# Ten dense weight units prepared in the experts and six in the dense stage, with two `sq` buffers, a later cast and three raw buffers

## The chip, the cores and the metric

The kernel runs on one core of one Trainium2 chip. The metric is device time in microseconds (us); below, a row's start is counted from the first instruction of the profiled execution. TensorE does the matrix products; VectorE, ScalarE and GpSimd the elementwise work; SyncE (SP) issues most transfers.

## What is computed

Three layers in a row, float32 results of shape (3072, 384): a gated linear attention over 4 x 8 heads, a mixture of eight experts of which each token goes to one, and a dense block with squared ReLU.

```python
for t in range(S):                                   # attention, per head
    state = alpha[:, :, t, :, None] * state + einsum('bhd,bhe->bhde', k[:, :, t], v[:, :, t])
    y[:, :, t] = einsum('bhd,bhde->bhe', q[:, :, t], state)
e_idx = argmax(x @ w_gate, axis=1)                   # experts, x is (3072, 384)
h = maximum(x[mask] @ w1[e], 0.0)                    # w1 (8, 384, 1024)
out[mask] = gate_w[mask, None] * eom[mask, e, None] * (h @ w2[e])
h = maximum(x @ w_in, 0.0)                           # dense, w_in (384, 2048)
out = (h * h @ w_out).astype(float32)                # w_out (2048, 384)
```

`w_in` and `w_out` arrive as float64 and are turned into pairs of float32 parts by integer operations in the kernel.

## The kernel before

Products that need more than one pass are made of three matmuls (`three`): both operands are split into a high part and a low part. Three stages follow each other on TensorE: the attention (to about 170 us), the experts (to 404 us) and the dense block.

The **experts** are 64 units, eight for each expert (`NU = E * NF`). In pass n of the loop TensorE runs `up1(n)` (the `ha` matmuls) and then `down1` of unit n-1 (the `acc` matmuls). ScalarE makes `hh` (L700) and VectorE `hl` (L703) from `ha`; `down1(n)` needs both. `fetch` brings a unit's raw weights by two transfers on SP's queue (L159, L160) into one of four raw buffers; `parts(m)` splits them by a cast on ScalarE (L170) and a subtraction on GpSimd (L171). Pass n prepares unit n+3 and then fetches the unit four behind that one, into the buffer that GpSimd has just read.

The **dense block** is 16 weight units over six blocks of 512 tokens. Since not all 16 units are ready when it starts, its passes are dealt to stretches (`SEGS`): block 0 with the first `NE` units, block 1 with all 16, block 0 with the rest, then blocks 2 to 5. Pass i of the loop runs `up2` (nine `ha` matmuls; then ScalarE's `r`, VectorE's `r`, ScalarE's `hh`, VectorE's `hl`, L928 to L934) and `down2` of pass i-2 (twelve `acc` matmuls). `split` makes the `xh` and `xl` of the next stretch (L913, L914): two of three at the middle of a stretch, the third in its last pass, on the queues ahead of that pass's `r`. At the end of the stretch over block 0, `finished` copies the four sums to `half` (L944, L946).

A dense unit is made ready by `dense_steps`, a generator of 18 steps: for each of two halves a load of `bits` (on SP's queue, two buffers) and eight steps of `wide_steps`, with one square and one cast on ScalarE (L1344, L1355) and seven VectorE operations (L1346 to L1363). The instructions are queued in the order of the program, and each engine works through its own queue in order. The generator `dense` prepares the first `NE` units: from pass 6 of the experts on, 18 x `NE` steps are dealt evenly to 57 passes, at the end of each. `late` prepares the others in the dense loop, between `up2` of pass i and `down2` of pass i-2, spread evenly over the first 22 passes (`need`).

Of the kernel before, what the change touches and what calls it, by code (L numbers as in the profile page):

```python
# [9 lines left out]
F32 = mybir.dt.float32  # L10
# [17 lines left out]
def moe_block_kernel(ctx: ExitStack, tc: tile.TileContext, q, k, v, alpha, w_gate, w_ogate,  # L28
                     w1, w2, w_in, w_out, out, dbg=None):
    nc = tc.nc  # L30
    B, H, S, D = q.shape
    NT, DM = out.shape
    E, _, FF = w1.shape
    FF2 = w_in.shape[1]
    P = 128
# [5 lines left out]
    NF2 = FF2 // P  # L41
    XW = 2 * D
    NU = E * NF
    GROUPS = [6, 6, 6, 3, 1, 1, 1]
    NRA = 4
    NRB = NF2 - 3
    NE = NF2 // 2
    BLK = 512
    NB = NT // BLK
    LAST = 2  # L50
    AHEAD = 6
# [11 lines left out]
    raw_p = fast.enter_context(tc.tile_pool(name="raw", bufs=2))  # L63
# [4 lines left out]
    with tc.manual_schedule():  # L68
# [66 lines left out]
        def source(n):  # L135
            if n < NU:
                e, f = divmod(n, NF)
                a, b = (w[bass.ds(expert[e], 1)].squeeze(0) for w in (w1, w2))
            else:
                f = n - NU  # L140
                a, b = w_in, w_out
            return (a[:, f * P:(f + 1) * P].rearrange("(k p) f -> p k f", p=P),
                    b[f * P:(f + 1) * P, :])
# [7 lines left out]
        def fetch(n):  # L151
            cols, rows_ = source(n)
            if n < NRA:
                if n % 2 == 0:
                    raws["pair"] = ring_b.tile([P, 4, DM], F32R, tag="w", name="raw").bitcast(F32)
                raw = raws["pair"][:, n % 2 * 2:n % 2 * 2 + 2, :]
            else:
                raw = (m2 if n % 4 >= 2 else raw_p).tile([P, 2, DM], F32, tag="raw", name="raw")
            nc.sync.dma_start(out=raw[:, 0, :].rearrange("p (k f) -> p k f", k=NK), in_=cols)  # L159
            nc.sync.dma_start(out=raw[:, 1, :], in_=rows_)  # L160
            raws[n] = raw
# [12 lines left out]
        def dense_steps(pool, first, last):  # L174


            halves = [(n, j) for n in range(first, last) for j in range(2)]
            loaded = {}

            def bring(i):  # L180
                if i < len(halves):
                    n, j = halves[i]
                    src = source(n)[j]
                    if w_in.dtype == F32:
                        raw = dst = pool.tile([P, DM], F32, tag="bits", name="bits")
                    else:
                        raw = pool.tile([P, DM, 2], I32, tag="bits", name="bits")
                        dst = raw.rearrange("p f o -> p (f o)")
                        src = src.bitcast(I32)
                    if j == 0:  # L190
                        dst = dst.rearrange("p (k f) -> p k f", k=NK)
                    nc.sync.dma_start(out=dst, in_=src)
                    loaded[i] = raw

            bring(0)
            for i, (n, j) in enumerate(halves):
                bring(i + 1)
                yield
                w = (unit_tile(n) if j == 0 else ring[n])[:, 2 * j:2 * j + 2, :]
                raw = loaded.pop(i)  # L200
                if w_in.dtype != F32:
                    yield from wide_steps(nc, pool, w, raw)
                    continue
                nc.scalar.copy(w[:, 0, :], raw)
                yield
                nc.vector.tensor_tensor(out=w[:, 1, :], in0=raw, in1=w[:, 0, :].bitcast(F32),
                                        op=ALU.subtract)
                yield
# [523 lines left out]
        def run(steps):  # L732
            for step in steps:
                step()
# [65 lines left out]
        i = NCH - 2  # L800
# [5 lines left out]
        for i, g in moving:  # L806
            x = xn.pop(i)
            nc.vector.tensor_scalar(x, x, g, None, op0=ALU.mult)
            scatter("xs", xs, idx[:, i:i + 1], x)
        i = NCH - 1  # L810
# [66 lines left out]
        m1 = moe.enter_context(tc.tile_pool(name="m1", bufs=1))  # L877
        m2 = moe.enter_context(tc.tile_pool(name="m2", bufs=2))
# [39 lines left out]

        SEGS = [(0, range(NE)), (1, range(NF2)), (0, range(NE, NF2))]
        SEGS += [(j, range(NF2)) for j in range(2, NB)]  # L920
# [54 lines left out]
        for n in range(NRA + 2, AHEAD + 2):  # L975
            fetch(n)
# [50 lines left out]

        dense = dense_steps(m2, NU, NU + NE)
        late = dense_steps(m2, NU + NE, NU + NF2)
        STEPS = 18  # L1030
# [3 lines left out]
        for n in range(NU):  # L1034
            e, f = divmod(n, NF)
            if f == 0 and e + 1 < E:
                choose(e + 1)
                gather(e + 1)
                if e == 0:
                    fetch(AHEAD + 2)  # L1040
                    fetch(AHEAD + 3)
            if f == 0 and e:
                offv[e] = nc.values_load(offi[0:1, e:e + 1], engines=[ACT], min_val=0,
                                         max_val=NT)
            if f == NF - 2:
                for kk in range(NK - 1):
                    if e + 1 < E:
                        turn(e + 1, kk)
                    else:
                        split(0, kk)  # L1050
            c = slice(EARLY if n < AHEAD else 0, WIDTHS[e])
            run(up1(n, c))
            if f == NF - 1:
                if e + 1 < E:
                    turn(e + 1, NK - 1)
            if n:
                down1(*last)
                m = n + NRA - 1 + sum(n < x for x in pauses)
                if n not in pauses and m < NU:
                    parts(m)  # L1060
                    if m + 4 < NU:
                        fetch(m + 4)
            last = n, c
            if n < NF - 2:
                for kk in range(NK):
                    part = slice(n * XP // (NF - 2), (n + 1) * XP // (NF - 2))
                    nc.gpsimd.memset(x2[:, kk, part], 0.0)
            if n == 2:
                next(dense)
            if n == 1:  # L1070
                sort()
            if n % 2 and n >= NU - 2 * NCH:
                i = (n - NU + 2 * NCH) // 2
                scatter("idl", idl, idx[:, i:i + 1], tok[:, i:i + 1])
            if n == 4:
                badb = judge()
            if n == 6:
                verdict(badb)
            if n >= AHEAD:
                k0, k1 = (STEPS * NE * (x - AHEAD) // (NU - 1 - AHEAD) for x in (n, n + 1))  # L1080
                for _ in itertools.islice(dense, k1 - k0):
                    pass
# [6 lines left out]


        seq = [(g, f) for g, (_, fs) in enumerate(SEGS) for f in fs]
        need = SEGS[0][1].stop + NF2 - 2
        for i, (g, f) in enumerate(seq):
            fs = SEGS[g][1]
            more = g + 1 < len(SEGS)
            if f == fs[len(fs) // 2] and more:
                for kk in range(NK - 1):
                    split(g + 1, kk)
            up2(g, f)
            if i < need:  # L1100
                k0, k1 = (STEPS * (NF2 - NE) * x // need for x in (i, i + 1))
                for _ in itertools.islice(late, k1 - k0):
                    pass
            if more or f < NF2 - LAST:
                if i > 1:
                    down2(*seq[i - 2])
# [232 lines left out]
def wide_steps(nc, pool, w, raw):  # L1339


    lo, hi = raw[:, :, 0], raw[:, :, 1]
    sq = pool.tile([w.shape[0], w.shape[2]], F32, tag="sq", name="sq", bufs=1)
    nc.scalar.activation(sq, hi.bitcast(F32), AF.Square)  # L1344
    yield
    nc.vector.scalar_tensor_tensor(out=hi.bitcast(F32), in0=sq, scalar=2.0 ** -30,  # L1346
                                   in1=hi.bitcast(F32), op0=ALU.is_ge, op1=ALU.mult)
    yield
    t = sq.bitcast(I32)
    nc.vector.tensor_scalar(t, hi, 3, 0x3FFFF000, op0=ALU.logical_shift_left, op1=ALU.bitwise_and)  # L1350
    yield
    nc.vector.scalar_tensor_tensor(out=t, in0=hi, scalar=-0x40000000, in1=t, op0=ALU.bitwise_and,
                                   op1=ALU.bitwise_or)
    yield
    nc.scalar.copy(w[:, 0, :], sq)  # L1355
    nc.vector.tensor_scalar(hi, hi, 0x1FF, 11, op0=ALU.bitwise_and, op1=ALU.logical_shift_left)
    yield
    nc.vector.scalar_tensor_tensor(out=lo, in0=lo, scalar=21, in1=hi, op0=ALU.logical_shift_right,
                                   op1=ALU.bitwise_or)
    yield  # L1360
    nc.vector.tensor_scalar(hi, t, -0x800000, None, op0=ALU.bitwise_and)
    yield
    nc.vector.scalar_tensor_tensor(out=w[:, 1, :], in0=lo, scalar=2.0 ** -31, in1=hi.bitcast(F32),  # L1363
                                   op0=ALU.mult, op1=ALU.mult)
    yield
# [31 lines left out]
```

## Time and profile before

| | |
|---|---|
| three runs | 831.48, 834.2, 836.35 us; median 834.2 |
| profiled execution | 830.97 us, span from first to last instruction 829.2 us |
| TensorE busy | 796.7 us (96%), 5215 matmuls |
| VectorE busy | 498.4 us (60%) |
| ScalarE busy | 381.3 us (46%) |
| GpSimd busy | 228.6 us (28%) |
| granted TensorE clock | 0.989 of full speed in the mean |

A row's time is from one execution. Matmuls are pipelined: the durations of neighbours overlap, and TensorE's pace is read from their starts. In brackets at the end of a row stand the idle time of the engine before that instruction and what ended it.

### The profile page before, as it was taken

The numbers are of one execution on the slowest core, as the hardware profiler recorded it, in microseconds if no ns is written. First come the engines' busy times: TensorE is split into PE (matmuls) and PEld (weight loads), VectorE is DVE, ScalarE is ACT, GpSimd is POOL, SyncE is SP. The second block draws the span as 40 slices with busy tenths as digits, with TensorE's granted clock in tenths as the row PEclk, the third lists the DMA queues.
The fourth block names the chain that finished last, engine by engine and source line by source line (L and its number), as shares of the span: only waits on it lengthen the run. The fifth ranks groups of instructions, "written<-read, shape, count | busy, mean of one in ns | idle before, by whom it ended". The sixth has DMA issues, their size and how long they took to land.

```text
span 829.2 us, 14100 instructions
## 1 busy us (share of the span) xinstructions
PE 796.7 (96%) x5215; PEld 731.1 (88%) x5215; DVE 498.4 (60%) x969; ACT 381.3 (46%) x734; POOL 228.6 (28%) x275
## 2 busy tenths in 40 slices
PE   7999999899999999999997999999999999999995
PEld 5899998798899999999986997999999999999995
DVE  8889999857355645876687787443333333333331
ACT  3677777554454555555444344332333333333221
POOL 3002341628456766777200000210002002002002
PEclk9999999899999999999998999999999999999998
DMA  9999994544554655674112110000000000000001
GB/s 135 179 210 180 209 175 99 185 132 157 156 161 128 182 149 152 167 181 127 39 58 76 58 58 21 39 13 27 0 1 39 1 1 38 1 1 39 1 0 42
DMA packets 153860, 74.98 MB, mean 90 GB/s; under 512 B 105406, under 2 KB 149430, under 8 KB 153782
## 3 DMA queue, kind: packets, MB, share of 16 engines
q1 hardware_dynamic: 149878, 64.52, 35.1%
q0 software_dynamic: 3904, 9.47, 3.1%
q8 instruction: 43, 0.70, 0.4%
q14 instruction: 35, 0.29, 0.1%
HBM read 61.76 MB, written 12.20 MB: 89 GB/s over the span
## 4 chain that ended last, share of the span: by engine, by line
PE 44%; issue 32%; DVE 14%; ACT 4%; POOL 3%; DMA 1%; SPq 1%; ACTq 0%; POOLq 0%; DVEq 0%
PE ha L1334 5%; PE ha L1336 5%; PE acc L1335 5%; PE acc L1334 5%; PE ha L1335 5%; PE acc L1336 5%; PE tr L268 3%; PE fx L425 2%; PE y L404 2%; POOL out_dram L129 2%; PE sc L337 2%; DVE r L929 2%; PE y L400 2%; ACT hh L933 2%; DVE bits L1346 1%
## 5 line engine op out<-in xcount | busy, mean ns | idle before, releaser
L1334 PE MATMUL ha<-xh,w 128*128 128x512 f32 (+7 forms) x456 | 173.9, 381 | 4.4 <-ACT xh L913 4.4
L1335 PE MATMUL ha<-xl,w 128*128 128x512 f32 (+7 forms) x456 | 172.3, 378 | 1.0 <-DVE xl L914 1.0
L1336 PE MATMUL ha<-xh,w 128*128 128x512 f32 (+7 forms) x456 | 172.5, 378 | 0.0
L929 DVE SCALAR_TENSOR_TENSOR r<-ha,r 128x512 f32<-128x512 f32 x96 | 66.3, 690 | 139.9 <-ACT r L928 137.6
L171 POOL TENSOR_TENSOR w<-raw,w 128x768 fp32r<-128x768 f32 x60 | 112.4, 1873 | 76.9 <-ACT w L170 73.9
L1334 PE MATMUL acc<-w,hh 128*128 128x384 f32 x384 | 130.6, 340 | 2.4 <-ACT half L946 1.8
L129 POOL DMA_INDIRECT out_dram<-o,ids x24 | 24.5, 1021 | 392.4 <-ACT o L954 359.8
L1336 PE MATMUL acc<-w,hl 128*128 128x384 f32 x384 | 130.6, 340 | 0.1
L1335 PE MATMUL acc<-w,hh 128*128 128x384 f32 x384 | 130.4, 340 | 0.0
L928 ACT ACTIVATE r<-ha 128x512 f32<-128x512 f32 x96 | 57.2, 596 | 144.4 <-PE ha L1336 144.3
L934 DVE TENSOR_TENSOR hl<-r,hh 128x512 fp32r<-128x512 f32 x96 | 66.6, 693 | 66.3 <-ACT hh L933 48.5
L1334 PEld LDWEIGHTS ha<-xh,w 128*128 128x128 f32 x456 | 85.9, 188 | 14.4 <-ACT xh L913 5.2
L1336 PEld LDWEIGHTS ha<-xh,w 128*128 128x128 f32 x456 | 85.8, 188 | 14.0
L933 ACT CAST hh<-r 128x512 fp32r<-128x512 f32 x96 | 59.5, 620 | 83.8 <-DVE r L929 82.6
L1335 PEld LDWEIGHTS ha<-xl,w 128*128 128x128 f32 x456 | 85.9, 188 | 11.6 <-DVE xl L914 1.9
L1334 PEld LDWEIGHTS acc<-w,hh 128*128 128x128 f32 x384 | 72.7, 189 | 7.3 <-ACT half L946 2.2
L170 ACT CAST w<-raw 128x768 fp32r<-128x768 f32 x64 | 53.5, 836 | 55.5 <-PE acc L1336 39.4
L1335 PEld LDWEIGHTS acc<-w,hh 128*128 128x128 f32 x384 | 72.7, 189 | 3.9
L1336 PEld LDWEIGHTS acc<-w,hl 128*128 128x128 f32 x384 | 72.7, 189 | 0.4 <-DVE hl L934 0.4
L703 DVE SCALAR_TENSOR_TENSOR hl<-ha,hh 128x448 fp32r<-128x448 f32 (+7 forms) x58 | 33.6, 580 | 54.8 <-ACT hh L700 52.3
L1334 PE MATMUL acc<-hh,w 128*128 128x448 f32 (+7 forms) x174 | 61.4, 353 | 0.0
L1335 PE MATMUL acc<-hl,w 128*128 128x448 f32 (+7 forms) x174 | 60.8, 350 | 0.1
(215 smaller groups left out, 1317.9 us busy)
## 6 DMA issues: line engine op xcount, KB each, us to landing
raw<-in_moe_w_dram SPq DMA_DIRECT2D x128, 192.0 KB
bits<-in_moe_w_in_dram SPq DMA_DIRECT2D x16, 384.0 KB
bits<-in_moe_w_out_dram SPq DMA_DIRECT2D x16, 384.0 KB
nat_al<-in_alpha_dram SPq DMA_DIRECT2D x24, 192.0 KB
nat_k<-in_k_dram SPq DMA_DIRECT2D x24, 192.0 KB
nat_q<-in_q_dram SPq DMA_DIRECT2D x24, 192.0 KB
nat_v<-in_v_dram SPq DMA_DIRECT2D x24, 192.0 KB
gx<-xs SPq DMA_DIRECT2D x22, 192.0 KB
```

The source lines that it names most:

```text
L129: ins = nc.gpsimd.indirect_dma_start(out=dst[:, :], out_offset=bass.IndirectOffsetOnAxis(ap=ix, axis=0), in_=src, in_offset=None)
L170: nc.scalar.copy(w[:, 0::2, :], raw)
L171: engine.tensor_tensor(out=w[:, 1::2, :], in0=raw, in1=w[:, 0::2, :].bitcast(F32), op=ALU.subtract)
L268: nc.tensor.transpose(ps[:, pr, :], src[:, pr, :], ident)
L703: nc.vector.scalar_tensor_tensor(out=hl, in0=ps, scalar=0.0, in1=hh.bitcast(F32), op0=ALU.max, op1=ALU.subtract)
L928: nc.scalar.activation(r, ps, AF.Relu)
L929: nc.vector.scalar_tensor_tensor(out=r, in0=ps, scalar=0.0, in1=r, op0=ALU.max, op1=ALU.mult)
L933: nc.scalar.copy(hh, r)
L934: nc.vector.tensor_tensor(out=hl, in0=r, in1=hh.bitcast(F32), op=ALU.subtract)
L1334: nc.tensor.matmul(ps, st[0], mv[0], start=start, stop=False)
L1335: nc.tensor.matmul(ps, st[0], mv[1], start=False, stop=False)
L1336: nc.tensor.matmul(ps, st[1], mv[0], start=False, stop=stop)
```

## The change

`NE`, the number of dense units prepared in the experts, goes from 8 to 10, and six are left to the dense loop. Their steps are dealt to 21 of the first 24 dense passes; passes 9, 10 and 11 (the end of the first stretch and the two behind it) get none. `sq` takes its pool's two buffers instead of one. The cast of `sq` to the weight's high part is queued two steps later. There are three raw buffers instead of four: two in `raw_p` and one in `m1`; the fetch goes three units ahead, and pass 0 fetches one unit less.

```diff
-    NE = NF2 // 2
+    NE = NF2 - 6
...
-                raw = (m2 if n % 4 >= 2 else raw_p).tile([P, 2, DM], F32, tag="raw", name="raw")
+                raw = (m1 if (n - NRA) % 3 == 2 else raw_p).tile([P, 2, DM], F32, tag="raw", name="raw")
...
                 if e == 0:
                     fetch(AHEAD + 2)
-                    fetch(AHEAD + 3)
...
                     parts(m)
-                    if m + 4 < NU:
-                        fetch(m + 4)
+                    if m + 3 < NU:
+                        fetch(m + 3)
...
-        need = SEGS[0][1].stop + NF2 - 2
+        spare_at = [i for i in range(NE + NF2 - 2) if i not in (NE - 1, NE, NE + 1)]
...
             up2(g, f)
-            if i < need:
-                k0, k1 = (STEPS * (NF2 - NE) * x // need for x in (i, i + 1))
+            if i in spare_at:
+                x = spare_at.index(i)
+                k0, k1 = (STEPS * (NF2 - NE) * y // len(spare_at) for y in (x, x + 1))
                 for _ in itertools.islice(late, k1 - k0):
                     pass
...
-    sq = pool.tile([w.shape[0], w.shape[2]], F32, tag="sq", name="sq", bufs=1)
+    sq = pool.tile([w.shape[0], w.shape[2]], F32, tag="sq", name="sq")
...
-    nc.scalar.copy(w[:, 0, :], sq)
     nc.vector.tensor_scalar(hi, hi, 0x1FF, 11, op0=ALU.bitwise_and, op1=ALU.logical_shift_left)
     yield
     nc.vector.scalar_tensor_tensor(out=lo, in0=lo, scalar=21, in1=hi, op0=ALU.logical_shift_right,
                                    op1=ALU.bitwise_or)
     yield
+    nc.scalar.copy(w[:, 0, :], sq)
     nc.vector.tensor_scalar(hi, t, -0x800000, None, op0=ALU.bitwise_and)
```

## Rows read from the trace of the kernel before

**Rows 1.** Stretches: TensorE, its weight loads, VectorE, ScalarE, GpSimd; clock, DMA.

```profile
360.00:400.00 40.00, 39.95 (x232) 39.56 (x232) 31.27 (x44) 21.22 (x38) 29.62 (x28) 1.00 0.51 137
400.00:440.00 40.00, 36.40 (x176) 31.34 (x174) 28.73 (x57) 17.44 (x33) 1.59 (x2) 0.99 0.20 50
520.00:560.00 40.00, 40.00 (x202) 36.23 (x202) 18.29 (x29) 14.33 (x25) 7.50 (x13) 1.00 0.07 30
```

**Rows 2.** TensorE's timeline, dense stage: start, duration, line, operation, idle before it.

```profile
410.39 0.34 PE L1334 MATMUL acc<-w,hh 128*128 128x384 f32 x1
...
427.97 0.44 PE L1334 MATMUL acc<-w,hh 128*128 128x384 f32 x1 [0.60 <-ACT hh L933]
...
439.03 0.79 PE L1334 MATMUL ha<-xh,w 128*128 128x512 f32 x1 [2.71 <-ACT xh L913]
...
453.88 0.45 PE L1334 MATMUL acc<-w,hh 128*128 128x384 f32 x1 [1.81 <-ACT half L946]
...
513.92 0.50 PE L1334 MATMUL ha<-xh,w 128*128 128x512 f32 x1 [1.66 <-ACT xh L913]
...
519.47 0.34 PE L1334 MATMUL acc<-w,hh 128*128 128x384 f32 x1
...
527.87 0.34 PE L1334 MATMUL acc<-w,hh 128*128 128x384 f32 x1
```

**Rows 3.** One stretch with a lower clock, columns as in rows 1.

```profile
439.00:445.90 6.90, 6.14 (x17) 5.35 (x18) 5.76 (x11) 2.74 (x6) 0.00 (x0) 0.51 0.18 57
```

**Rows 4.** VectorE's timeline, dense stage: first `r`, a split, one whole half.

```profile
407.02 0.69 DVE L929 SCALAR_TENSOR_TENSOR r<-ha,r 128x512 f32<-128x512 f32 x1 [4.72 <-ACT r L928]
...
439.81 0.69 DVE L914 TENSOR_TENSOR xl<-x,xh 128x512 fp32r<-128x512 f32 x1
...
454.73 0.69 DVE L929 SCALAR_TENSOR_TENSOR r<-ha,r 128x512 f32<-128x512 f32 x1 [0.38 <-ACT r L928]
456.11 0.69 DVE L934 TENSOR_TENSOR hl<-r,hh 128x512 fp32r<-128x512 f32 x1 [0.69 <-ACT hh L933]
456.72 0.55 DVE L1346 SCALAR_TENSOR_TENSOR bits<-sq,bits 128x384 f32<-128x384 f32 x1
...
459.69 0.56 DVE L1363 SCALAR_TENSOR_TENSOR w<-bits 128x384 fp32r<-128x384 int32 x1
460.16 0.68 DVE L929 SCALAR_TENSOR_TENSOR r<-ha,r 128x512 f32<-128x512 f32 x1
```

**Rows 5.** ScalarE's timeline at the end of the first dense stretch.

```profile
437.94 0.51 ACT L1355 CAST w<-sq 128x384 fp32r<-128x384 f32 x1 [1.62 <-DVE sq L1352]
438.36 0.61 ACT L913 CAST xh<-x 128x512 fp32r<-128x512 f32 x1
```

**Rows 6.** Timelines of four engines in the last expert.

```profile
387.03 0.52 ACT L1355 CAST w<-sq 128x384 fp32r<-128x384 f32 x1 [2.44 <-DVE sq L1352]
387.96 0.55 DVE L703 SCALAR_TENSOR_TENSOR hl<-ha,hh 128x376 fp32r<-128x376 f32 x1 [0.57 <-issue]
388.19 0.33 PE L1334 MATMUL acc<-hh,w 128*128 128x376 f32 x1
388.57 0.44 PE L1335 MATMUL acc<-hl,w 128*128 128x376 f32 x1
390.30 0.83 ACT L170 CAST w<-raw 128x768 fp32r<-128x768 f32 x1 [1.27 <-issue]
391.21 1.85 POOL L171 TENSOR_TENSOR w<-raw,w 128x768 fp32r<-128x768 f32 x1 [0.53 <-ACT w L170]
391.28 2.20 DVE L1363 SCALAR_TENSOR_TENSOR w<-bits 128x384 fp32r<-128x384 int32 x1
393.42 0.83 ACT L170 CAST w<-raw 128x768 fp32r<-128x768 f32 x1 [1.12 <-PE acc L1336]
```

**Rows 7.** A fetch on SP's queue, and the stretch in which its data was in.

```profile
350.31 0.39 SPq L159 DMA_DIRECT2D raw<-in_moe_w_dram  x1
354.00:355.00 1.00, 1.00 (x7) 1.00 (x7) 1.00 (x3) 0.99 (x3) 0.85 (x3) 1.00 0.49 168
```

## Prediction

> **What bounds the kernel now.** I read the table of stretches first. TensorE is all but full in the last experts (39.95 of 40 us) and in the late dense blocks (40.00 of 40, 202 matmuls), and falls behind in the early dense stage: 176 matmuls from 400 to 440 [rows 1]. So the question is what holds TensorE in the first 24 or so dense units, called slots here (slot i is the i-th pass of the dense loop). VectorE is the engine that stands out there: 28.73 of 40 us busy, against 18.29 later [rows 1].
>
> The timeline of TensorE gives the size. A slot is nine `ha` and twelve `acc` matmuls. Two slots lie between the `acc` starts at 519.47 and 527.87, so an undisturbed slot takes 4.20 us. Between the `acc` starts at 410.39 (slot 0's) and 519.47 (slot 23's) lie 23 slots: 109.1 us, where 23 x 4.20 = 96.6 would do. **12.5 us are lost**, and the rows with idle time say where: 0.60 at 427.97 (`hh` late), 2.71 at 439.03 (`xh` late, the end of the first stretch), 1.81 at 453.88 (the four `half` evictions late), 1.66 at 513.92 (`xh`, the end of the second stretch) [rows 2]. The stall at 439 has a second price: for the following 6.9 us the granted clock is 0.51, the lower level (1.2 GHz), and 17 matmuls run in that time where 6.9 us at 202 in 40 us would hold 35 [rows 1, 3]. The engine had stood idle 2.7 us just before; after the idle 1.8 and 1.7 us it kept the clock. So this one place costs about 6.3: 2.71, and 18 matmuls too few at 0.2 (0.76 idle for `xl` among it). The rest of the 12.5 is slower first matmuls after each stop.
>
> Why they are late is in VectorE's timeline. A slot costs it `r`, a wait of 0.69 for ScalarE's `hh`, and `hl`: 454.73 to 456.72, 1.99 us. Then come the conversion steps of later weight units. One half of a unit is nine steps with seven VectorE operations, 456.72 to 460.16: 3.44 us, 0.49 each [rows 4]. Before, the 144 late steps are spread over 22 slots: 6.55 steps, 5.09 operations, 2.50 us, so a slot needs 4.49 us of VectorE against TensorE's 4.20, before any split (`xl`, 0.69 each) or eviction. The queue falls behind from slot 0 on and everything behind it (split, eviction, `hl`) comes late. ScalarE is drawn in: its cast of `sq` sat 1.62 us on VectorE at 437.94, and the split's `xh` stood right behind it [rows 5].
>
> **Part by part.** *Ten units early, six late.* The late work falls from 144 steps to 108, that is 84 VectorE operations, 41 us. *No steps in slots 9, 10, 11.* They are dealt to 21 of 24 slots: 5.14 steps, 4.0 operations, 1.97 us, so a slot needs 1.99 + 1.97 = 3.96 us, under 4.20. I follow the queue from the first `r` at 407.02 [rows 4]. Slots 0 to 8 have 46 steps, 35.8 operations, 17.5 us; nine times 1.99 is 17.9; two `xl` at slot 5 add 1.3. So slot 9's split can start at 443.7 and its `xl` is done at 444.4. TensorE at full pace starts slot 10's `ha` at 410.39 + 2.1 + 7 x 4.20 = 441.9 and wants the third `xl` 1.6 later, 443.5. That stop stays, with some 0.9 us instead of 6.3; I take 0.9, bounds 0 and 2.7 (today's stop without the clock). On the way `hl` has room: slot 5's is done at 429.9 and wanted at 410.39 + 5 x 4.20 = 431.4. With slots 9 to 11 empty VectorE gets back up to 5.9 us, so the `half` copies of slot 11 stand behind nothing and the 1.81 goes. In the second stretch there is 0.24 us to spare in each slot, and slot 24 has no steps, so the stop at 513.92 goes too. Dense stage: -12.5 + 0.9 = **-11.6 us**, with -12.5 and -9.8 as bounds.
>
> *What the two units cost in the experts.* 36 steps more (180 for 144 over the same 57 units, 3.16 a unit for 2.53): 28 VectorE operations, eight of ScalarE (0.52 each, in an engine busy 21 of 40 us), four loads of 384 KB (some 7 GB/s on 137, share 0.51) [rows 1, 6]. ScalarE and the loads have cover. VectorE is the doubtful one: it is 31.27 of 40 us busy in the last experts [rows 1], and its conversion operations wait for GpSimd. The one at 391.28 took 2.20 us, where the same line takes 0.56 in the dense stage, while GpSimd's 1.85 us subtraction from 391.21 ran; `hl`, which reads PSUM, kept its 0.55 at 387.96 [rows 4, 6]. TensorE is already at its edge: that `hl` came at 388.51, and the matmul that reads it started at 388.57, 0.38 after its neighbour, where 232 in 40 us make 0.17 [rows 1, 6].
> The Trainium skill, SBUF — State Buffer, section Who interferes with whom, states this as a rule that speaks against the change: a VectorE instruction with two SBUF inputs, or in a two-port mode, and a GpSimd instruction that reads SBUF shut each other out for a whole instruction. The trace agrees (2.20 for 0.56). By it a moved operation costs more in the experts, where GpSimd works, than in the dense stage, where it rests.
> Bounds from rows: at 0.49 us the added operations of the last three experts (24 units of some 3.12 us [rows 6], 0.49 operation each: 12) are 5.8 us, and VectorE has 8.7 of 40 us idle, 16 over these 75 us: cost 0. At the blocked price of 2.20 they are 26 us against the 16: 10. I take **+2.0**, nearer to 0: between two of GpSimd's operations there is 3.12 - 1.85 = 1.27 us, room for two or three conversion operations, and 3.16 steps are 2.46; an `hl` is pushed to the edge at times, a few tenths each. A gain is nearly excluded, since TensorE loses only 0.05 of 40 us there.
>
> *Cast queued later, two `sq` buffers.* Both take waits out of ScalarE's queue: the cast that sat 2.44 us at 387.03 with the next `hh` behind it [rows 6], and the square that had to wait for the previous half. The work is the same; this is what lets me count +2.0 and not more, and it is part of the -11.6. Alone 0.
>
> *Three raw buffers.* A fetch goes out once GpSimd is done with the buffer's last unit, now three units ahead instead of four. The SP queue stands on that wait, with gathers and `bits` loads behind it, as it does now. From cast to GpSimd's end are 2.76 us (390.30 to 393.06), the next use is 3 x 3.12 = 9.4 after the cast, so 6.6 us are left to land [rows 6]. The slowest fetch that I found, issued at 350.31 behind some slow microseconds, was in by 355, 4.7 us [rows 7]. Cost 0. If that cover goes, ScalarE's cast waits with `hh` behind it.
>
> **Sum**: -11.6 + 2.0 = **-9.6 us**. The profiled execution took 830.97 us (span 829.2, 1.8 around it), so 821.4 like for like; the median of the three runs shown is 3.2 higher, and with the same difference **824.6**.
>
> **Rivals.**
> 1. *VectorE's idle time in the experts can't be used* (in each unit it waits in order for `hh`). Then the 12 operations of the last three experts cost their 5.8 us: -11.6 + 5.8 = -5.8, **828.4**. For it: the `hl` at the edge; against: TensorE idles 0.05 of 40 us.
> 2. *The end of the first stretch stays as bad*: slots 7 and 8 still have steps right before slot 9's split; if the queue comes 2 us later than in my sum, the clock falls again. Then 6.3 of the 12.5 stay: -6.2 + 2.0 = -4.2, **830.0**. Against: 3.96 is under 4.20, and stops of under 2 us left the clock alone.
> 3. *All is hidden*: -12.5, **821.7**.
> 4. *Slower: the moved operations meet GpSimd.* Place: last three experts; price 2.20 us for each operation that stands in front of an `hl` with no idle time left. From the sixth on (11.6 / 2.20) the gain is gone; with all 12, 26 us, it is +14.8, **849**. It is what the Trainium skill's rule (SBUF — State Buffer, Who interferes with whom) would do at its worst. For it: 2.20 for 0.56; against: three operations fit between two of GpSimd's.
> 5. *The raw buffers come late*: with 8.0 us to land, a unit takes (8.0 + 2.76) / 3 = 3.59 us for 3.12, on the last 24 units +11, and with the other terms +1.4: **836**. Against: 4.7 was the worst.
>
> **How the numbers follow.** Forecast 0.60 (alone 821.5 to 828), rival 1 0.14, rival 2 0.10, rival 3 0.08, rival 4 0.05, rival 5 0.03. The range reaches from a little under rival 3 to rival 2: 820.5 to 830.5. 0.5% (4.2 us, about what a measurement of this kernel can tell from no change) puts the line at 830.0: faster are the forecast, rivals 1 and 3, 0.82; rival 2 lies on the line and rival 5 inside it, 0.13; slower is rival 4, 0.05.
>
> **What would show it.** Right: 200 or more matmuls in each 40 us from 405 on, no granted clock under 1.00 around 440, VectorE's `r` no more than 5 us behind its `ha`, an idle of about 0.9 us before slot 10's third `xl` at 443, none at the evictions; in the last experts `hl` closer to its matmul and TensorE's idle time 1 to 3 us. Wrong: idle TensorE between 300 and 400 of more than 5 us; ScalarE's cast of `raw` waiting for a load; a low clock after 440.

## The result and the profile after

Six runs of each kernel: 819.56 us in the median (818.27 to 827.59) against 833.29 (831.48 to 836.35); the ratio is 0.9851, with a 95% interval of 0.9814 to 0.9887 (it is not the ratio of the two medians, which is 0.9835). The forecast was -9.6 us (824.6 of 834.2, a ratio of 0.9885); the medians differ by 13.7 us, the two profiled executions by 11.5 (819.47 and 830.97). Against these six runs of before the median lies 0.9 us under the lower end of the range; against the three that stood ahead of the prediction the ratio makes it 821.8.

The stretches of the kernel after, columns as in [rows 1]:

```profile
360.00:400.00 40.00, 40.00 (x233) 39.70 (x232) 35.04 (x49) 22.84 (x41) 31.72 (x28) 1.00 0.61 159
400.00:440.00 40.00, 40.00 (x202) 36.04 (x201) 29.16 (x57) 17.08 (x33) 1.60 (x2) 1.00 0.20 50
440.00:480.00 40.00, 40.00 (x203) 36.20 (x202) 27.91 (x53) 17.88 (x33) 0.00 (x0) 1.00 0.13 40
...
520.00:560.00 40.00, 40.00 (x203) 36.26 (x202) 16.96 (x27) 13.46 (x23) 7.99 (x16) 1.00 0.10 40
```

TensorE is full in all of them. Where 176 matmuls ran from 400 to 440 before [rows 1] there are now 202, with VectorE as busy as it was. In the last experts VectorE rose from 31.27 to 35.04 of 40 us, and TensorE took no notice.

Four starts on TensorE's timeline divide the time: the third expert's first transposes, the first `ha` of the dense stage, and the `acc` of slots 0 and 23, as in [rows 2]:

```profile
227.46 0.38 PE L902 MATMUL tx<-ident,gx 128*128 128x128 f32 x2
...
404.87 0.40 PE L1336 MATMUL ha<-xh,w 128*128 128x512 f32 x1
...
411.17 0.34 PE L1336 MATMUL acc<-w,hh 128*128 128x384 f32 x1
...
507.75 0.34 PE L1336 MATMUL acc<-w,hh 128*128 128x384 f32 x1
```

From the first to the second are 177.41 us; before they were 177.37 (226.73 to 404.10). From the third to the fourth are 96.58 us for 23 slots of 4.20, so **the dense stage loses nothing where it lost 12.5**. In this execution the experts begin 0.73 us later than in that of before; 0.61 of that is there at 163 us already, in the attention. -12.49 + 0.73 + 0.04 is the 11.7 by which the span fell (829.2 to 817.5). These two measures, "experts" (177.1 is the shortest of any kernel here) and "dense loss" (start of slot 23's `acc` less that of slot 0's, less 96.6), are read from every kernel below. Each is of one execution; how well they repeat is seen from 177.4 in four kernels and 0.0 in five.

### The profile page after: what moved, and what is told of

Its sections match the earlier page's. It is cut to its first block, busy times and chain, and to the rows that moved or that the text cites. A ratio compares the mean times of both kernels' runs of the same rounds, so it can differ in the third digit from the quotient of the medians.

```text
span 817.5 us, 14112 instructions
## 1 busy us (share of the span) xinstructions
PE 798.3 (98%) x5215; PEld 735.1 (90%) x5215; DVE 515.8 (63%) x969; ACT 381.6 (47%) x734; POOL 230.1 (28%) x275
## 4 chain that ended last, share of the span: by engine, by line
PE 59%; issue 31%; DVE 4%; POOL 3%; ACT 2%; DMA 0%; SPq 0%; POOLq 0%; ACTq 0%; DVEq 0%
PE ha L1336 7%; PE ha L1338 7%; PE ha L1337 7%; PE acc L1336 7%; PE acc L1337 7%; PE acc L1338 7%; PE tr L268 4%; PE fx L425 3%; PE sc L337 3%; PE y L404 2%; POOL out_dram L129 2%; PE y L400 2%; PE tx L902 1%; PE u L378 1%; DVE sp L303 1%
## 5 line engine op out<-in xcount | busy, mean ns | idle before, releaser
L171 POOL TENSOR_TENSOR w<-raw,w 128x768 fp32r<-128x768 f32 x60 | 114.3, 1904 | 74.6 <-ACT w L170 73.6
L1336 PE MATMUL acc<-hh,w 128*128 128x448 f32 (+7 forms) x174 | 61.4, 353 | 0.0
L1338 PE MATMUL acc<-hh,w 128*128 128x448 f32 (+7 forms) x174 | 60.7, 349 | 0.0
```

What stands on the lines that cost most here:

```text
L171: engine.tensor_tensor(out=w[:, 1::2, :], in0=raw, in1=w[:, 0::2, :].bitcast(F32), op=ALU.subtract)
L1336: nc.tensor.matmul(ps, st[0], mv[0], start=start, stop=False)
L1338: nc.tensor.matmul(ps, st[1], mv[0], start=False, stop=stop)
```

## The experiments

All are the changed kernel with one part of it altered. The two times are of the profiled execution, the ratio is of the timed runs to those of before on the same chip.

| kernel | units early | experts, us | dense loss, us | ratio (95% interval) |
|---|---|---|---|---|
| before | 8 | 177.4 | 12.5 | |
| after | 10 | 177.4 | 0.0 | 0.9851 (0.9814 to 0.9887) |
| the two ScalarE edits, not the units | 8 | 177.1 | 8.8 | 0.9951 (0.9933 to 0.9970) |
| the units, not the ScalarE edits | 10 | 178.7 | 1.8 | 0.9887 (0.9871 to 0.9904) |
| steps in every slot | 10 | 177.4 | 0.8 | 0.9843 (0.9827 to 0.9860) |
| one `sq` buffer | 10 | 177.4 | 0.8 | 0.9832 (0.9801 to 0.9863) |
| cast early | 10 | 178.7 | 1.0 | 0.9854 (0.9821 to 0.9886) |
| nine units, steps in every slot | 9 | 177.5 | 3.9 | 0.9922 (0.9894 to 0.9950) |
| twelve units | 12 | 186.3 | 0.0 | 0.9998 (0.9971 to 1.0026) |
| thirteen units | 13 | 196.6 | 0.0 | 1.0056 (1.0029 to 1.0083) |
| thirteen units, no subtraction | 13 | 177.1 | 0.0 | one run, 837.2 us, not compared |
| two raw buffers | 10 | 188.7 | 0.0 | 1.0021 (0.9994 to 1.0049) |

### The ScalarE edits alone, and the units alone

Theory A: VectorE's time in a slot against TensorE's 4.20 us decides. Theory B: ScalarE's waits for VectorE made the stops.

```diff
-    NE = NF2 - 6
+    NE = NF2 - 8
...
-        spare_at = [i for i in range(NE + NF2 - 2) if i not in (NE - 1, NE, NE + 1)]
+        spare_at = list(range(NE + NF2 - 2))
```

> Eight units early and the late steps spread evenly over 22 slots as before; the later cast, the second sq buffer and the three raw buffers stay. Theory A (VectorE's time per slot decides): a slot still needs 1.99 + 2.50 = 4.49 us of VectorE against 4.20, so the queue falls behind by 0.3 us a slot; only the 1.6 to 1.8 us stops of ScalarE behind VectorE are gone. TensorE idles at the two stretch ends again, 6 to 11 us lost, time about 826 to 831. Theory B (ScalarE's waits made the stops, VectorE's share did not): no idle TensorE in the dense stage, time about 820.

```diff
-    sq = pool.tile([w.shape[0], w.shape[2]], F32, tag="sq", name="sq")
+    sq = pool.tile([w.shape[0], w.shape[2]], F32, tag="sq", name="sq", bufs=1)
...
+    nc.scalar.copy(w[:, 0, :], sq)
     nc.vector.tensor_scalar(hi, hi, 0x1FF, 11, op0=ALU.bitwise_and, op1=ALU.logical_shift_left)
...
-    nc.scalar.copy(w[:, 0, :], sq)
     nc.vector.tensor_scalar(hi, t, -0x800000, None, op0=ALU.bitwise_and)
```

> The change without its two edits in ScalarE's queue: ten units early, no steps in slots 9 to 11, three raw buffers, but the cast early and one sq buffer. Theory A: 3.96 us a slot fit, so the dense stage stays nearly free (0 to 2 us lost). In the experts the early cast waits for VectorE again, as it did at 387.03; if that is what had eaten the slack of hl, the two more units now cost TensorE 1 to 4 us there, time about 821 to 825. Theory B: the dense stops come back, 6 to 12 us, time 826 to 832.

With the ScalarE edits alone the stops are the old ones, at the old places, but for the wait for `hh` (0.60 before), which is gone. TensorE's timeline of that kernel, the rows with idle time:

```profile
435.48 0.49 PE L1336 MATMUL ha<-xh,w 128*128 128x512 f32 x1 [2.52 <-ACT xh L913]
...
437.00 0.80 PE L1337 MATMUL ha<-xl,w 128*128 128x512 f32 x1 [1.02 <-DVE xl L914]
...
449.25 0.45 PE L1336 MATMUL acc<-w,hh 128*128 128x384 f32 x1 [0.52 <-ACT half L946]
...
508.55 0.50 PE L1337 MATMUL ha<-xl,w 128*128 128x512 f32 x1 [0.31 <-DVE xl L914]
```

The 2.5 us before the third `xh` are the 2.71 of [rows 2], and the clock falls behind it again: from 437 to 442.5 the granted clock is 0.50. The idle time before the evictions and at the second stretch end fell by some 1.3 us each. So 12.5 became 8.8: A, with a part for B. With the units alone the dense stage lost 1.8, all before one `xl`, and the experts 1.3 (0.8 before the first row below, the rest in small delays of `hl` between 332 and 336):

```profile
400.21 0.44 PE L1337 MATMUL acc<-hl,w 128*128 128x376 f32 x1 [0.56 <-DVE hl L703]
...
442.88 0.50 PE L1337 MATMUL ha<-xl,w 128*128 128x512 f32 x1 [1.58 <-DVE xl L914]
```

ScalarE's timeline of the same kernel shows where the 0.8 comes from: as in [rows 6] the early cast sits on VectorE's operation, which stands behind one that was itself held up (1.86 us from 391.54). The split's `xh` and the next `hh` stand behind the cast, and VectorE's `xl` and the last `hl` come late in turn.

```profile
394.75 0.52 ACT L1357 CAST w<-sq 128x384 fp32r<-128x384 f32 x1 [2.54 <-DVE sq L1354]
395.17 1.14 ACT L913 CAST xh<-x 128x512 fp32r<-128x512 f32 x2
396.21 0.48 ACT L700 ACTIVATE hh<-ha 128x376 fp32r<-128x376 f32 x1
```

Together the four kernels make a square: without and with the ScalarE edits 12.5 and 8.5 us are lost with eight units (8.8 dense, less 0.3 in the experts), 3.1 and 0.0 with ten. The units with their slots are worth 8.5 to 9.4, the ScalarE edits 3.1 to 4.0. One corner, the kernel before, also has the fourth raw buffer; that was not undone alone.

### Which of the two ScalarE edits, and the empty slots

Each was undone alone, by its line in the diff above; in the third kernel the late steps go to all 24 slots, by the `spare_at` line of the first.

> The change with one sq buffer instead of two; the later cast stays. Of the 1.3 us in the experts and 1.8 us at the end of the first dense stretch that came back without both ScalarE edits, this one gets the share of the square, which waits for the previous half's last use of sq. If the square's wait is what matters: 1 to 3 us lost, mostly at the stretch end (slot 8 to 10). If the cast's wait is: 0 to 0.5 us.

> The change with the cast queued early, right behind the third VectorE operation; the two sq buffers stay. If the cast's wait for VectorE is what brought hl late in the experts: TensorE stops there (1 us or more between 330 and 402) and at slot 8 to 10, together near 3 us. If the square's wait is what matters: 0 to 0.5 us.

> The change with the 108 late steps spread over all 24 slots, none of them empty: 4.5 steps, 3.5 operations, 1.72 us, 3.71 us of VectorE in a slot. Theory A: slots 0 to 8 get lighter, so slot 9's split comes about 2 us earlier than in the change; behind it the evictions of slot 11 have 1.7 us of steps ahead of them, which the slack bears: no idle TensorE, time about 820. If the empty slots are what saves the stretch end: 2 to 7 us lost there, time 822 to 827.

One `sq` buffer costs 0.8 us at slot 8 and nothing in the experts; I had expected 1 to 3, or 0 to 0.5. The early cast costs 1.0 at slot 8 and 1.3 in the experts. So the cast alone makes the experts' 1.3 of both edits undone, and the two add up to about the 1.8 at slot 8. The empty slots save 0.8, where I had expected nothing or 2 to 7: without them the stretch end is free and the evictions stop TensorE for 0.2 and 0.6 us instead. The timed runs can't tell these three from the change (the intervals overlap); the traces can.

### Nine units

```diff
-    NE = NF2 - 6
+    NE = NF2 - 7
...
-        spare_at = [i for i in range(NE + NF2 - 2) if i not in (NE - 1, NE, NE + 1)]
+        spare_at = list(range(NE + NF2 - 2))
```

> The change with nine units early and seven late, the late steps spread evenly over 23 slots: 126 steps, 5.48 a slot, 4.26 operations, 2.09 us, so 4.08 us of VectorE in a slot, just under TensorE's 4.20. Theory A (the sum against 4.20 decides): a slot behind schedule only through the two xl of the middle and the third xl at the end, 0.5 to 3 us lost, mostly at slot 8 to 11, time 13 to 9 us under before. If it is the number of moved units that counts in proportion (8 early lost 8.8 with both ScalarE edits, 10 none): 4.4 us lost.

```profile
437.54 0.50 PE L1337 MATMUL ha<-xl,w 128*128 128x512 f32 x1 [1.06 <-DVE xl L914]
...
447.76 0.44 PE L1336 MATMUL acc<-w,hh 128*128 128x384 f32 x1 [1.09 <-ACT half L946]
...
449.98 0.44 PE L1336 MATMUL acc<-w,hh 128*128 128x384 f32 x1 [0.91 <-DVE half L944]
```

3.9 us are more than I expected of 4.08 against 4.20, and nearer to the proportion (4.4). A slot that just fits is not enough. TensorE runs the `ha` of slots 0 to 2 in 6.3 us before its first `acc`, while VectorE needs over 12 for three slots, so it starts with a debt; then come two `xl`, one more, and two `half` copies, and 0.12 us a slot pays too little of it back by slot 11. The debt can be read from the timelines. VectorE's `r` of slot 2 starts 3.8 us after the end of that slot's `ha` in this kernel, in the change and with steps in every slot alike. At slot 8 it is 4.6 us here, though TensorE has stopped once by then, 3.0 in the change (3.96 us a slot) and 1.6 with steps in every slot (3.71). That is theory A, taken with the debt. The loss in proportion to the units fits the number as well, and this one run does not rule it out.

### How many units the experts bear

```diff
-    NE = NF2 - 6
+    NE = NF2 - 3
```

> The change with 13 units early and three late. 4.11 steps, 3.2 conversion operations in each expert unit. Theory C (the conversion operations fit between GpSimd's operations, two or three a unit, and cost nothing until these places are full): now they don't fit, hl comes behind a blocked operation in most of the last 24 units, TensorE loses 0.2 to 0.7 us in each, 5 to 15 us between 320 and 405, time about 825 to 835. Theory D (VectorE has idle time enough, blocked or not): no idle TensorE in the experts, time about 820.

> The change with twelve units early and four late: 3.79 steps, 2.95 conversion operations in each expert unit. Theory C (two to three fit between two operations of GpSimd at no cost): at the edge, the experts from the third expert's first transposes to the dense stage take 2 to 12 us more than the 177.4 of both kernels. If thirteen units lost their 19 us by something that only they do: 0 to 1 us.

The whole experts stage of before, of after, with twelve and with thirteen units, columns as in [rows 1], one fence for each kernel:

```profile
226.70:404.10 177.40, 177.35 (x977) 172.13 (x975) 114.09 (x169) 95.08 (x167) 117.90 (x98) 1.00 0.57 151
```

```profile
227.50:404.90 177.40, 177.40 (x977) 172.10 (x976) 139.81 (x197) 98.72 (x174) 119.52 (x97) 1.00 0.60 160
```

```profile
228.00:414.00 186.00, 181.84 (x976) 172.64 (x974) 162.78 (x221) 101.46 (x181) 119.07 (x98) 0.99 0.62 161
```

```profile
226.00:421.00 195.00, 183.47 (x966) 174.50 (x966) 166.89 (x230) 101.49 (x182) 116.85 (x98) 0.97 0.60 155
```

28 operations more keep VectorE busy for 25.7 us more, 0.92 each, where they took 0.49 in the dense stage. At 139.8 of 177.4 us TensorE still waits for nothing; with twelve units the experts grow by 8.9 us and with thirteen by 19.2, more than the 5 to 15 expected and more than the whole gain of the change. Theory C has the edge right, between ten and twelve units (eleven was not tried), but not its reason. The conversion operations don't find places between GpSimd's that then fill up: 24 of 98 took over 0.7 us in this stage before, 33 of 124 after, 43 of 148 with twelve units and 41 of 161 with thirteen, about a quarter each time. So some 0.8 to 0.9 us each is their price from the start, and VectorE's idle time bears it, up to 139.8 of 177.4 us in this stage, and no longer at 162.8 of 186. With thirteen TensorE waits for `hl`, and in two places for a split:

```profile
315.86 0.45 PE L1337 MATMUL acc<-hl,w 128*128 128x404 f32 x1 [2.42 <-DVE hl L703]
...
336.62 0.45 PE L1337 MATMUL acc<-hl,w 128*128 128x392 f32 x1 [2.05 <-DVE hl L703]
...
360.18 0.69 PE L1337 MATMUL ha<-xl,w 128*128 128x384 f32 x1 [2.99 <-DVE xl L905]
...
403.01 0.44 PE L1337 MATMUL acc<-hl,w 128*128 128x376 f32 x1 [2.02 <-DVE hl L703]
```

The clock took its share: 0.97 in the mean, with stretches at the lower level behind such stops.

### Is it GpSimd that makes the moved operations dear?

```diff
             nc.scalar.copy(w[:, 0::2, :], raw)
+            if n >= AHEAD:
+                return
             engine.tensor_tensor(out=w[:, 1::2, :], in0=raw, in1=w[:, 0::2, :].bitcast(F32),
                                  op=ALU.subtract)
```

Beside it the expert matmuls of these units take the high part of the weight where they took the low one.

> Thirteen units early as before, but GpSimd's subtraction of the expert units 6 to 63 is left out; the matmuls that read the low part of these weights read the high part instead, so as many matmuls run and the output is another. Theory F (VectorE's conversion operations wait for GpSimd's subtraction): no conversion operation takes over 0.9 us, 3.2 operations are 1.6 us in a unit of 3.1, and the experts are back at 177 to 179 us from the third expert's first transposes instead of 196.6. Theory G (VectorE's own work and its waits for ScalarE fill the units): they stay above 190.

The stage again, and one conversion line in it; first the stretch without the subtraction:

```profile
246.00:423.00 177.00, 177.00 (x977) 172.17 (x976) 111.13 (x233) 102.56 (x184) 0.54 (x2) 1.00 0.57 173
```

then the line without it and, in the kernel of thirteen units above, with it (count: shortest/median/longest in ns):

```profile
L1359 DVE TENSOR_SCALAR bits<-bits x21: 349/362/367, 238.7 to 396.8; 128x384 int32<-128x384 int32 x21
```

```profile
L1357 DVE TENSOR_SCALAR bits<-bits x20: 360/1746/2087, 237.3 to 399.9; 128x384 int32<-128x384 int32 x20
```

Theory F. With 13 units the experts are back at 177.1 us, no conversion operation takes longer than 0.57, and VectorE is less busy (111.1 us) than in the kernel before with eight. What made the moved work dear was GpSimd's subtraction: of the unit's work only that was left out, with its hold on the raw buffer. The run's whole time (837.2 us) says nothing, because in this kernel TensorE stood idle for 17 us ahead of the stage. With its queue free, GpSimd sent its 24 `idl` scatters in one burst (194 to 233 us), and beside it ScalarE waited for a load of `bits`; that the burst delayed the load was not tested:

```profile
ACT sq L1348 <- DMA bits<-in_moe_w_in_dram: 16.2, 2, 13.1
```

(waits from 180 to 240: us in total, times, the longest.)

### Two raw buffers

```diff
-                raw = (m1 if (n - NRA) % 3 == 2 else raw_p).tile([P, 2, DM], F32, tag="raw", name="raw")
+                raw = raw_p.tile([P, 2, DM], F32, tag="raw", name="raw")
...
-                if e == 0:
-                    fetch(AHEAD + 2)
...
-                    if m + 3 < NU:
-                        fetch(m + 3)
+                    if m + 2 < NU:
+                        fetch(m + 2)
```

> The change with two raw buffers, the fetch going two units ahead. Between a buffer's release by GpSimd and ScalarE's next cast from it lie 2 x 3.12 - 2.76 = 3.5 us in the last expert and some 4.6 in the widest. Theory E (a fetch takes up to 4.7 us to land): the casts wait up to 1.2 us for a load, hl behind them is late, 2 to 12 us lost in the experts. If loads land in under 3 us nearly always: 0 to 1 us, and the three buffers of the change have plenty to spare.

ScalarE's waits for loads in the experts from 230 to 400, first after, then with two buffers:

```profile
ACT w L170 <- DMA raw<-in_moe_w_dram: 2.8, 2, 1.4
```

```profile
ACT w L170 <- DMA raw<-in_moe_w_dram: 36.0, 19, 4.8
```

With two, the loads hold up 19 casts and the experts take 11.3 us more: theory E. The issue of the load that held up a cast longest, and that cast:

```profile
274.30 0.34 SPq L160 DMA_DIRECT2D raw<-in_moe_w_dram  x1
```

```profile
280.13 0.83 ACT L170 CAST w<-raw 128x768 fp32r<-128x768 f32 x1 [4.83 <-DMA raw<-in_moe_w_dram]
```

So that load took up to 5.8 us. The view counts the whole wait to a load that came last, though a part of each is for TensorE. With three buffers a load was the last thing a cast waited for twice. The issue of the slower one, its cast, and the end of the matmuls for which the cast waits too:

```profile
275.36 0.34 SPq L160 DMA_DIRECT2D raw<-in_moe_w_dram  x1
```

```profile
281.10 0.83 ACT L170 CAST w<-raw 128x768 fp32r<-128x768 f32 x1 [1.40 <-DMA raw<-in_moe_w_dram]
```

```profile
280.45 0.35 PE L1338 MATMUL acc<-hh,w 128*128 128x412 f32 x1
```

This load took up to 5.7 us. Of the 1.4 us all but some 0.3 is the wait for TensorE, which ended at 280.80. So the three buffers of the change aren't far from their edge, but TensorE lost nothing by them.

## Why the prediction was right, and where its sum was off

**The 12.5 us and their cause** held. All of it was there to be had, at the places named, and the clock kept its upper level (1.00 around 440) once the stop at the stretch end was gone. VectorE's `r`, up to 7.6 us behind its `ha` before, is never more than 4.1 behind. That VectorE's time in a slot decides is shown by the units alone (12.5 to 1.8 dense) against the ScalarE edits alone (12.5 to 8.8).

**The stop at the end of the first stretch** was forecast at 0.9 us, and is 0. VectorE's timeline of the kernel after at the split, then TensorE's where it is used:

```profile
443.39 0.68 DVE L914 TENSOR_TENSOR xl<-x,xh 128x512 fp32r<-128x512 f32 x1
444.00 0.68 DVE L929 SCALAR_TENSOR_TENSOR r<-ha,r 128x512 f32<-128x512 f32 x1
```

```profile
444.31 0.40 PE L1337 MATMUL ha<-xl,w 128*128 128x512 f32 x1
```

From the first `r` (407.80) to this `xl` are 35.6 us, in which VectorE stands idle for `hh` alone, as the sum had it. My sum had 36.7: 46 steps hold 35 operations and not 35.8, and in the slots these take 0.47 us each and not 0.49, since the `r` behind them starts some 0.1 before the last one's end, after every three to six operations and not after seven. The `xl` was done at 444.07 for a matmul at 444.31. The term was right to a microsecond, and a microsecond was all there was: with the early cast or one `sq` buffer the stop is 0.8 to 1.0, with both undone 1.8. That slots 9 to 11 are empty is worth 0.8, at the evictions.

**The two units in the experts** were forecast at +2.0 and cost 0.0. That operations are held up by GpSimd was right, as the run without its subtraction shows: in the kernel after all 30 conversion operations that started well inside a subtraction ended 0.2 to 0.4 us after it. The Trainium skill's rule (SBUF — State Buffer, Who interferes with whom) agrees with these rows. The row of `hl` that I gave for PSUM, 387.96, shows nothing, since no subtraction ran beside it. One of the kernel after does, by the timelines of GpSimd and VectorE: `hl` keeps its 0.55 beside a subtraction, and the conversion operation behind it takes 1.74.

```profile
365.61 1.86 POOL L171 TENSOR_TENSOR w<-raw,w 128x768 fp32r<-128x768 f32 x1 [1.06 <-ACT w L170]
```

```profile
365.68 0.55 DVE L703 SCALAR_TENSOR_TENSOR hl<-ha,hh 128x384 fp32r<-128x384 f32 x1
366.14 1.74 DVE L1365 SCALAR_TENSOR_TENSOR w<-bits 128x384 fp32r<-128x384 int32 x1
```

Three sizes were off. An operation costs VectorE 0.92 us there, between my 0.49 and 2.20. VectorE could use its idle time, which rival 1 doubted. And I credited the later cast with nothing here beyond "not more" than 2.0: by the run with the early cast it is worth 1.3 of them, since `xh` and `hh` no longer stand behind a cast that stands behind GpSimd. `hl` still comes at the last moment, as expected, by TensorE's timeline:

```profile
366.04 0.34 PE L1336 MATMUL acc<-hh,w 128*128 128x384 f32 x1
366.28 0.45 PE L1337 MATMUL acc<-hl,w 128*128 128x384 f32 x1
```

This `hl` ended at 366.23, and its matmul came 0.24 after its neighbour instead of 0.17. So rival 3, all hidden, is what happened; I had given it 0.08, too little beside a forecast that stood 2.9 us from it. Rival 4's mechanism is real, but its edge lies further on: twelve units bring it about.

**The raw buffers** cost nothing, as forecast, but with less to spare than I thought. The 4.7 us were not the slowest landing: the load above took up to 5.7. A cast of `raw` that waits for a load was among my signs of being wrong; it came twice, for some 0.3 us each, and cost TensorE nothing.

## What to carry to other kernels

Where an engine's queue feeds the one that bounds the kernel, add up its time for one pass, with the waits that its order forces on it, against the bound's pace, and count the debt it starts with: a pass that only just fits (4.08 of 4.20) still lost 3.9 us. Work moved out of such a stage has another price where it lands; there, count what it shares with the engines that run beside it, and look for the point where the slack ends: two units were free, four cost over two thirds of the gain (8.9 of 12.5). A small instruction on a third engine that waits for the busy one is worth queuing later, so that nothing stands behind its wait.

## What the runs showed of the hardware

A VectorE operation of 0.36 us in SBUF took 1.75 us in the median with GpSimd's subtraction in the unit (thirteen units early), and 0.36 without it. `hl`, which reads PSUM, kept its time: in the kernel after 0.53 to 0.63 us in all 51, 17 of which started inside a subtraction. And transfers can take longer than the rows of a quiet stretch show: with thirteen units loads of `raw` (192 KB) landed in 2.5 to 5.4 us and loads of `bits` (384 KB) in 3.7 to 6.1, as far as the profile tells, and beside the burst of indirect scatters one of `raw` took 20.1 and ScalarE waited 13 us for one of `bits`.
